# A gated feed-forward layer: four units instead of eight on the leading quarter, and the same four on the second

## The chip, the cores and the metric

The kernel runs on one core of a Trainium2 chip. The metric is the device time of one execution in microseconds (us). Before the change the median of three runs is 299.8 us (299.75 to 299.83).

The engines that matter are TensorE (PE in the profile; PEld are its weight loads), VectorE (DVE), ScalarE (ACT), GpSimd (POOL) and SyncE (SP). SP, ACT and POOL also issue DMAs; each has a queue of its own.

## The reference

`x` is 1024 tokens by 1024, `w_gate` and `w_up` are 1024 by 3584, `w_down` is 3584 by 1024, all in bf16:

```python
def _gelu(x):
    return jax.nn.gelu(x, approximate=True)

def reference(x, w_gate, w_up, w_down):
    return (_gelu(x @ w_gate) * (x @ w_up)) @ w_down
```

## The kernel before, in words

**The work.** The 3584 hidden columns are 28 units of 128. For a unit and a range of tokens, TensorE adds up eight steps over the inner dimension (k 0 to 7), once with gate weights (G) and once with up weights (U). Such a pair is a *part* (list `parts`, line 136). When its G and U are complete, ACT puts the GELU of G into one of four buffers `tb` (line 443), and VectorE multiplies it by U from PSUM into `hT` (line 483). When all units are done, the second product runs 17 jobs over the 28 units (line 421), and ACT and VectorE copy the result out.

**The opening.** The first product needs x with the inner dimension on the partitions, so x is transposed on the chip. Three ways are used:
- Tokens 0 to 255 (`XA`) come as two loads `xa`, one on SP's and one on ACT's queue (line 293). TensorE transposes k 0 to 4 through the identity (`turn_xa`, line 345), ACT copies these from PSUM into `xT` in the four pieces of `XA_PS` (line 436), and VectorE transposes k 5 to 7 in 16 instructions of 32 partitions by 192 (line 459).
- Tokens 256 to 383 (`XB1`), 384 to 511 (`XB2`) and 512 to 1023 (`XC2`) are loaded in runs of 512 bytes into `xs` (line 284), each in four DMAs of 32 partitions, two on SP (side 0) and two on ACT (side 1). VectorE transposes them, one k at a time (line 474).

Units 0 to 7 open together on tokens 0 to 255: eight parts of 256 tokens, one PSUM bank each, walked k by k, so that every k needs one gate and one up piece of 128 rows by 1024 columns (`load_w0`, line 288, 16 DMAs of 256 KB in runs of 2 KB, all on SP). Then the same eight units run on tokens 256 to 511: units 0 to 3 walk k together, its first four k in two strips of 128 tokens, then units 4 to 7 go one after the other. After that come units 0 to 7 on tokens 512 to 1023, and units 8 to 27 on both halves of 512 tokens, one part after the other, each with two PSUM banks.

**Weights after the opening.** They come in groups of four units (`groups`, line 109), 1 MB of gate on SP and 1 MB of up on POOL (`load_w`, line 275), in runs of 1 KB. There are three places for a group: `lo` and `hi`, the two halves of the wide buffer `big` that holds units 0 to 7 at first, and `small`. The first group waits in `gate_w` (line 304) until the last 512 tokens of x have landed, a later one until the units whose place it takes are done. `w_down` is loaded in seven pieces of 1 MB between them (`issue_wd`).

**What sets the order.** Everything is written out by hand: `steps` (line 157) is TensorE's order of multiplications, `dve_order` (line 187) is VectorE's, where `E` is the multiplication of a part and A, B, C and D are the transposes of XB1, XB2, XC2 and the whole of 256 to 511 for one k. ACT's and SP's programs are their loops. An engine works through its list in order, so that a wait in it holds what stands behind. On SP these are `xa`, the 16 first weight pieces, a wait for the up piece of k 5, its six x loads, then the groups. ACT issues `xa`, makes its copies, waits for the same up piece and issues its six x loads; its GELUs stand behind that. `HOLD` (line 132) adds one wait of TensorE for the gate piece of k 7.

Of the kernel before, what the change touches and what calls it, by code (L numbers as in the profile page):

```python
# [5 lines left out]
P = 128  # L6
BF16 = mybir.dt.bfloat16
FP32 = mybir.dt.float32
ACTF = mybir.ActivationFunctionType
# [75 lines left out]
def bass_standalone__geglu_ffn__sampling_kernel(  # L85
# [23 lines left out]
    groups = [(8, 4, "s"), (12, 4, "lo"), (16, 4, "hi"), (20, 4, "s"), (24, 4, "lo")]  # L109
    assert groups[-1][0] + groups[-1][1] == FM  # L110
    NG = len(groups)
    war = [None, 3, 7, 11, 15]
    slot_of = {m: ("lo" if m < GSZ else "hi", m % GSZ, None) for m in range(NBIG)}
# [17 lines left out]
    XA_PS = [(3, 0, 1, 0, 1), (7, 0, 1, 1, 2), (4, 1, 3, 0, 2), (5, 3, 5, 0, 2)]  # L131
    HOLD = ((6, "U", 5), ("wg", 7))
    XA_DVE = (5, 8)
# [3 lines left out]
    for t0, t1 in (XA, XB):  # L137
        for m in range(NBIG):
            parts.append((m, t0, t1, (m, 0, 256), (m, 256, 512)))
    NSHORT = len(parts)  # L140
    rest = [(m, 1) for m in range(NBIG)] + [(m, h) for m in range(NBIG, FM) for h in range(NH)]
    for n, (m, h) in enumerate(rest):
        b = 2 * (n % 4)
        parts.append((m, h * 512, h * 512 + 512, (b, 0, 512), (b + 1, 0, 512)))
# [29 lines left out]
    for key, ps_ in (("G", (0, 1, 2, 6, 3, 7, 4)), ("U", (0, 1, 2, 3)), ("G", (5,)), ("U", (7, 6, 4, 5))):  # L174
        steps += [(p, key, 0, None) for p in ps_]
    together(range(0, 8), 1, 6)
    for half in (range(0, 4), range(4, 8)):
        together(half, 6, 7)
        one_by_one(half, 7)
    together(range(8, 12), 0, 4, XB1)  # L180
    together(range(8, 12), 0, 4, XB2)
    together(range(8, 12), 4, 6)
    one_by_one(range(8, 12), 6)
    one_by_one(range(12, NPART), 0)
# [3 lines left out]
    mix = ("E0 E1 E2 A0 E3 A1 A2 A3 B0 B1 B2 B3 E4 D4 D5 E5 D6 D7 E6 E7 "  # L188
           "C0 E8 C1 E9 C2 E10 E11 C3 C4 E12 C5 E13 C6 C7 E14 E15")
# [5 lines left out]
    dve_order += [("E", p) for p in range(NSHORT, NPART)]  # L195
# [26 lines left out]
    Q_W0 = {(w, k): _Clock(f"{w}0k{k}", 16) for k in range(DK) for w in ("wg", "wu")}  # L222
# [10 lines left out]
    with ExitStack() as es:  # L233
# [54 lines left out]
        def load_w0(ew, eng, w, k):  # L288
            ctx.set((w + "0", k), ew.do(lambda: eng.dma_start(  # L289
                big[w][:, k, :], w_r[w][:, k, 0:NBIG * P]), clock=Q_W0[(w, k)]))  # L290

        def early_loads(ew, eng, side):
            ctx.set(("xa", side), ew.do(lambda: eng.dma_start(  # L293
                xa[:, side, :], xa_r[:, side, :]), clock=Q_XA[side]))
            yield
            if side == 0:
                for k in range(DK):
                    for w in ("wg", "wu"):
                        load_w0(ew, eng, w, k)
            ew.wait(Q_W0[("wu", 5)], ctx.get(("wu0", 5)))  # L300
            for q in XPIECES:
                load_x(ew, eng, q, side)

        def gate_w(ew, j):
            if war[j] is None:
                for s in range(2):
                    ew.wait(Q_X[(XC2, s)], ctx.get(("x", XC2, s)))
                return -1
            ew.wait(C_PE, ctx.get(("U", last_part[war[j]])))
            return war[j]  # L310

        def prog_pool(eng):
            pool = _Eng(ctx, eng, C_POOL)
            v = pool.do(lambda: eng.iota(diff[:, :], pattern=[[1, P]], base=0, channel_multiplier=-1))
            pool.wait(C_POOL, v)
            ctx.set("ident", pool.do(lambda: eng.tensor_scalar(
                ident[:, :], diff[:, :], 0.0, None, ALU.is_equal)))
            wd_mine = [k for k in range(len(wd_groups)) if k % 2 == 1]
            for j in range(NG):
                known_chunk = gate_w(pool, j)  # L320
                load_w(pool, eng, "wu", j)
                issue_wd(pool, eng, wd_mine, known_chunk, Q_WD_POOL)
            issue_wd(pool, eng, wd_mine, FM, Q_WD_POOL, force=True)
            ctx.set("wd_pool_total", Q_WD_POOL.n)

        def prog_sp(eng):
            sp = _Eng(ctx, eng, None)
            for _ in early_loads(sp, eng, 0):
                pass
            wd_mine = [k for k in range(len(wd_groups)) if k % 2 == 0]  # L330
            for j in range(NG):
# [26 lines left out]
        def part_step(pe, eng, opened, i, key, dk, tok):  # L358
# [6 lines left out]
            if j is None:  # L365
                pe.wait(Q_W0[(w, dk)], ctx.get((w + "0", dk)))
# [12 lines left out]
            if (i, key, dk) == HOLD[0]:  # L379
                pe.wait(Q_W0[HOLD[1]], ctx.get((HOLD[1][0] + "0", HOLD[1][1])))  # L380
# [48 lines left out]
        def prog_act(eng):  # L429
            act = _Eng(ctx, eng, C_ACT)  # L430
            act.do(lambda: eng.activation(warm[:, 0:1], const0, ACTF.Gelu_apprx_tanh))
            for _ in early_loads(act, eng, 1):
                for j, (bank, k0, k1, b0, b1) in enumerate(XA_PS):
                    act.wait(C_PE, ctx.get(("XP", j)))
                    nt = P * (b1 - b0)
                    ctx.set(("XA", j), act.do(lambda: eng.activation(  # L436
                        xT[:, k0:k1, P * b0:P * b1],
                        ps[:, bank, 0:nt * (k1 - k0)].rearrange("p (k t) -> p k t", t=nt), ACTF.Copy)))
            for i, (m, t0, t1, (gb, g0, g1), us) in enumerate(parts):
                act.wait(C_PE, ctx.get(("U" if us[0] == gb else "G", i)))  # L440
# [100 lines left out]
```

## Time and profile before

| what | us or share |
|---|---|
| median of three runs | 299.8 |
| the profiled execution | 299.5 |
| its span in the profile | 298.2 |
| TensorE busy | 295.0 (99%) |
| VectorE busy | 64.2 (22%) |
| ACT busy | 42.3 (14%) |
| first multiplication with weights starts | 4.85 |
| units 0 to 7 are through tokens 0 to 255 | 19.37 |
| units 0 to 7 are through tokens 256 to 511 | 33.42 |
| second product starts | 199.18 |

Times inside the profile count from the start of its span. Matmuls overlap their neighbours, so the distance between two starts, and not the length of one, is what a matmul costs. A line of the timeline gives start, length, engine, line of the kernel, operation, tiles and how many instructions were merged; in brackets stands the idle time before it and what ended it. In the rows by stage, the busy time of PE, PEld, DVE, ACT and POOL is followed by the clock, the mean share of the 16 DMA engines and GB/s. A DMA's landing is counted from its issue.

### The profile page before, as it was taken

What the parts mean: (1) busy time and instruction counts of PE and PEld (TensorE: products, weight loads), DVE (VectorE), ACT (ScalarE), POOL (GpSimd) and SP (SyncE); (2) the same over time, 40 slices, a digit from 0 to 9 for tenths busy, and PEclk for the clock granted to TensorE, in tenths of its full rate; (3) what the DMA queues carried; (4) which work ended last, traced back from release to release, by engine and by line L of the source; (5) the groups of instructions that cost most, each with busy time, mean ns of one, the idle gap of its engine ahead of it and who ended that gap; (6) DMA issues with size and microseconds to landing.
All of it is one profiled execution on the core that took longest, in us unless ns stands there. A gap on an engine that the chain in (4) does not pass through costs nothing.

```text
span 298.2 us, 3516 instructions
## 1 busy us (share of the span) xinstructions
PE 295.0 (99%) x1552; PEld 148.9 (50%) x1552; DVE 64.2 (22%) x108; ACT 42.3 (14%) x79; POOL 7.8 (3%) x14
## 2 busy tenths in 40 slices
PE   8999999999999999999999999999999999999997
PEld 5889644444444444444444444444444444444446
DVE  4669721111122111122111122110000000000000
ACT  4032211121111121111121111110000000000000
POOL 1001001020000002001000000000000000000000
DMA  7988004856009301943104000000000100010001
GB/s 256 393 198 266 19 2 138 284 191 235 0 0 297 127 0 29 370 166 99 44 0 141 0 2 0 0 0 20 18 18 20 35 18 18 20 35 18 18 20 35
DMA packets 17806, 26.43 MB, mean 89 GB/s; under 512 B 1024, under 2 KB 11392, under 8 KB 17792
## 3 DMA queue, kind: packets, MB, share of 16 engines
q1 hardware_dynamic: 13840, 16.78, 17.0%
q0 software_dynamic: 2176, 8.39, 8.0%
q10 hardware_dynamic: 1776, 1.05, 1.3%
q8 instruction: 12, 0.20, 0.3%
q14 instruction: 2, 0.02, 0.0%
HBM read 24.12 MB, written 2.10 MB: 88 GB/s over the span
## 4 chain that ended last, share of the span: by engine, by line
PE 94%; DMA 3%; SPq 2%; issue 0%; ACT 0%
PE ps L384 61%; PE ps L421 32%; DMA wubig<-in_w_up_dram 3%; SPq L289 2%; SPq L293 0%; ACT xT L449 0%
## 5 line engine op out<-in xcount | busy, mean ns | idle before, releaser
L421 PE MATMUL ps<-wd,hT 128*128 128x512 bf16 (+1 forms) x476 | 96.9, 367 | 0.0
L384 PE MATMUL ps<-xT,wgbig 128*128 128x512 bf16 (+2 forms) x400 | 79.8, 337 | 0.2 <-DMA wgbig<-in_w_gate_dram 0.2
L384 PE MATMUL ps<-xT,wubig 128*128 128x512 bf16 (+2 forms) x400 | 79.8, 337 | 0.2
L421 PEld LDWEIGHTS ps<-wd,hT 128*128 128x128 bf16 x476 | 46.5, 98 | 50.5
L483 DVE TENSOR_TENSOR hT<-tb,ps 128x512 bf16<-128x512 f32 (+1 forms) x64 | 38.9, 613 | 136.6 <-PE ps L384 136.6
L443 ACT ACTIVATE tb<-ps 128x512 f32<-128x512 f32 (+1 forms) x64 | 34.1, 544 | 158.5 <-PE ps L384 157.0
L384 PEld LDWEIGHTS ps<-xT,wubig 128*128 128x128 bf16 x400 | 38.0, 98 | 32.2 <-DMA wubig<-in_w_up_dram 0.7
L384 PEld LDWEIGHTS ps<-xT,wgbig 128*128 128x128 bf16 x400 | 38.0, 98 | 31.6 <-DMA wgbig<-in_w_gate_dram 0.3
L384 PE MATMUL ps<-xT,wusmall 128*128 128x512 bf16 x128 | 30.2, 379 | 0.0
L384 PE MATMUL ps<-xT,wgsmall 128*128 128x512 bf16 x128 | 30.2, 379 | 0.0
L489 DVE CAST xT<-ps 128x512 bf16<-128x512 f32 (+1 forms) x8 | 5.3, 658 | 88.1 <-PE ps L421 88.1
L384 PEld LDWEIGHTS ps<-xT,wusmall 128*128 128x128 bf16 x128 | 12.5, 98 | 15.1
L384 PEld LDWEIGHTS ps<-xT,wgsmall 128*128 128x128 bf16 x128 | 12.5, 98 | 15.1
L449 ACT ACTIVATE xT<-ps 128x512 bf16<-128x512 f32 (+1 forms) x9 | 5.2, 573 | 93.1 <-PE ps L421 93.1
L474 DVE STREAM_TRANSPOSE xT<-hT 128x128 bf16<-128x128 bf16 (+2 forms) x20 | 13.3, 706 | 0.0
L459 DVE STREAM_TRANSPOSE xT<-hT 32x192 bf16<-32x192 bf16 x16 | 8.2, 514 | 4.6 <-DMA hT<-in_x_dram 4.1
L278 POOL DMA_DIRECT2D wubig<-in_w_up_dram x3 | 2.7, 884 | 63.4 <-PE ps L384 63.4
L398 PE MATMUL ps<-const-bfloat16-1.0 128*128 128x512 bf16 (+1 forms) x10 | 3.1, 502 | 0.8 <-PEq L526 0.8
L278 POOL DMA_DIRECT2D wusmall<-in_w_up_dram x2 | 2.0, 990 | 47.2 <-PE ps L384 26.0
L272 POOL DMA_DIRECT2D wd<-in_w_down_dram x3 | 2.3, 762 | 19.1 <-PE ps L384 19.1
L398 PEld LDWEIGHTS ps<-const-bfloat16-1.0 128*128 128x128 bf16 x10 | 1.3, 142 | 2.4 <-issue 2.4
L436 ACT ACTIVATE xT<-ps 128x128 bf16<-128x128 f32 (+1 forms) x4 | 1.5, 438 | 1.9 <-PE ps L351 1.8
(10 smaller groups left out, 4.4 us busy)
## 6 DMA issues: line engine op xcount, KB each, us to landing
wd<-in_w_down_dram SPq DMA_DIRECT2D x4, 1024.0 KB, 11.3
wgbig<-in_w_gate_dram SPq DMA_DIRECT2D x3, 1024.0 KB, 5.7
wubig<-in_w_up_dram POOLq DMA_DIRECT2D x3, 1024.0 KB, 9.8
wd<-in_w_down_dram POOLq DMA_DIRECT2D x3, 1024.0 KB, 11.5
wgbig<-in_w_gate_dram SPq DMA_DIRECT2D x8, 256.0 KB, 5.5
wubig<-in_w_up_dram SPq DMA_DIRECT2D x8, 256.0 KB, 5.7
wgsmall<-in_w_gate_dram SPq DMA_DIRECT2D x2, 1024.0 KB, 6.1
wusmall<-in_w_up_dram POOLq DMA_DIRECT2D x2, 1024.0 KB, 9.7
```

What stands on the lines that cost most here:

```text
L272: ew.do(lambda: eng.dma_start(wd[:, a:b, :], wd_r[:, a:b, :]), clock=clock)
L278: ctx.set((w, j), ew.do(lambda: eng.dma_start(wbuf(w, buf)[:, :, 0:gsz * P], w_r[w][:, :, c0 * P:(c0 + gsz) * P]), clock=q))
L289: ctx.set((w + "0", k), ew.do(lambda: eng.dma_start(big[w][:, k, :], w_r[w][:, k, 0:NBIG * P]), clock=Q_W0[(w, k)]))
L384: v = pe.do(lambda: eng.matmul(ps[:, bank, f0:f1], wbuf(w, buf)[:, dk, slot * P:(slot + 1) * P], xT[:, dk, t0:t1], start=first, stop=last ...
L398: pe.do(lambda: eng.matmul(ps[:, 0, 0:n], ones_w, ones_x[:, 0:n], start=True, stop=True), mark=False)
L421: v = pe.do(lambda: eng.matmul(ps[:, b, 0:ncols], hT[:, m, tc * P:(tc + 1) * P], wd[:, m, col0:col0 + ncols], start=(m == 0), stop=(m == F ...
L443: ctx.set(("A", i), act.do(lambda: eng.activation(t_bufs[i % NTB][:, 0:t1 - t0], ps[:, gb, g0:g1], ACTF.Gelu_apprx_tanh)))
L449: ctx.set(("E", ji), act.do(lambda: eng.activation(osb[:, tc, col0:col0 + ncols], ps[:, b, 0:ncols], ACTF.Copy)))
L459: v = dve.do(lambda: eng.transpose(xT[32 * a:32 * (a + 1), XA_DVE[0]:XA_DVE[1], XA[0]:XA[1]].rearrange("p k (b t) -> p k b t", t=P)[:, :, ...
L474: v = dve.do(lambda: eng.transpose(xT[:, dk, q[0]:q[1]].rearrange("p (c i) -> p c i", i=32), src))
L483: ctx.set(("D", i), dve.do(lambda: eng.tensor_tensor(hT[:, m, t0:t1], t_bufs[i % NTB][:, 0:t1 - t0], ps[:, ub, u0:u1], ALU.mult)))
L489: ctx.set(("E", ji), dve.do(lambda: eng.tensor_copy(osb[:, tc, col0:col0 + ncols], ps[:, b, 0:ncols])))
```

## The change

Four units open instead of eight. Units 0 to 3 run on tokens 0 to 255 in PSUM banks 0 to 3, then on tokens 256 to 511 in banks 4 to 7; of these only k 0 is in two strips of 128 tokens. Units 4 to 7 have no short parts any more: they run on tokens 0 to 511 whole, one part after the other. Then the order goes on as before.

The first weights are 512 columns wide, for four units, in runs of 1 KB, and come in five pieces of gate and of up each: k 0, k 1, k 2-3, k 4-5 and k 6-7. Units 4 to 7 become a group of their own (index 0, place `hi`), with gate and up both on SP, right behind SP's pieces of XB1 and XB2 and ahead of its pieces of XC2. SP has no wait in this stretch any more. ACT waits for the gate piece of k 4-5, issues its pieces of XB1 and XB2, and issues those of XC2 after its first four GELUs. TensorE transposes k 0 to 6 of the first tokens (14 instead of 10 transposes, with a fifth piece in bank 6 for ACT to copy), and VectorE only k 7. `HOLD` is gone, and `dve_order` is written anew. POOL begins with group 1.

```diff
-    groups = [(8, 4, "s"), (12, 4, "lo"), (16, 4, "hi"), (20, 4, "s"), (24, 4, "lo")]
+    groups = [(4, 4, "hi"), (8, 4, "s"), (12, 4, "lo"), (16, 4, "hi"), (20, 4, "s"), (24, 4, "lo")]
-    war = [None, 3, 7, 11, 15]
+    war = [None, None, 3, 7, 11, 15]
...
-    XA_PS = [(3, 0, 1, 0, 1), (7, 0, 1, 1, 2), (4, 1, 3, 0, 2), (5, 3, 5, 0, 2)]
-    HOLD = ((6, "U", 5), ("wg", 7))
-    XA_DVE = (5, 8)
+    XA_PS = [(3, 0, 1, 0, 1), (7, 0, 1, 1, 2), (4, 1, 3, 0, 2), (5, 3, 5, 0, 2), (6, 5, 7, 0, 2)]
+    XA_DVE = (7, 8)
+    W0 = [(0, 1), (1, 2), (2, 4), (4, 6), (6, 8)]
...
-    for t0, t1 in (XA, XB):
-        for m in range(NBIG):
-            parts.append((m, t0, t1, (m, 0, 256), (m, 256, 512)))
+    for t0, t1, b0 in (XA + (0,), XB + (GSZ,)):
+        for m in range(GSZ):
+            parts.append((m, t0, t1, (b0 + m, 0, 256), (b0 + m, 256, 512)))
...
-    rest = [(m, 1) for m in range(NBIG)] + [(m, h) for m in range(NBIG, FM) for h in range(NH)]
+    rest = [(m, 0, 512) for m in range(GSZ, NBIG)] + [(m, 512, 1024) for m in range(NBIG)]
+    rest += [(m, h * 512, h * 512 + 512) for m in range(NBIG, FM) for h in range(NH)]
...
-    for key, ps_ in (("G", (0, 1, 2, 6, 3, 7, 4)), ("U", (0, 1, 2, 3)), ("G", (5,)), ("U", (7, 6, 4, 5))):
-        steps += [(p, key, 0, None) for p in ps_]
-    together(range(0, 8), 1, 6)
-    for half in (range(0, 4), range(4, 8)):
-        together(half, 6, 7)
-        one_by_one(half, 7)
-    together(range(8, 12), 0, 4, XB1)
-    together(range(8, 12), 0, 4, XB2)
-    together(range(8, 12), 4, 6)
-    one_by_one(range(8, 12), 6)
-    one_by_one(range(12, NPART), 0)
+    for k0, k1 in W0:
+        for key in ("G", "U"):
+            for dk in range(k0, k1):
+                steps += [(p, key, dk, None) for p in range(GSZ)]
+    together(range(GSZ, NSHORT), 0, 1, XB1)
+    together(range(GSZ, NSHORT), 0, 1, XB2)
+    together(range(GSZ, NSHORT), 1, DK)
+    one_by_one(range(NSHORT, NPART), 0)
...
-    mix = ("E0 E1 E2 A0 E3 A1 A2 A3 B0 B1 B2 B3 E4 D4 D5 E5 D6 D7 E6 E7 "
-           "C0 E8 C1 E9 C2 E10 E11 C3 C4 E12 C5 E13 C6 C7 E14 E15")
+    mix = ("A0 B0 D1 D2 E0 D3 E1 D4 E2 D5 E3 D6 D7 E4 E5 E6 E7 "
+           "C0 C1 E8 C2 C3 E9 C4 C5 C6 E10 C7 E11")
...
+        def load_w0(ew, eng, w, i):
+            k0, k1 = W0[i]
+            ctx.set((w + "0", i), ew.do(lambda: eng.dma_start(
+                wbuf(w, "lo")[:, k0:k1, :], w_r[w][:, k0:k1, 0:GSZ * P]), clock=Q_W0[(w, i)]))
...
-            for _ in early_loads(sp, eng, 0):
-                pass
+            load_xa(sp, eng, 0)
+            for i in range(len(W0)):
+                for w in ("wg", "wu"):
+                    load_w0(sp, eng, w, i)
+            load_x(sp, eng, XB1, 0)
+            load_x(sp, eng, XB2, 0)
+            load_w(sp, eng, "wg", 0)
+            load_w(sp, eng, "wu", 0)
+            load_x(sp, eng, XC2, 0)
             wd_mine = [k for k in range(len(wd_groups)) if k % 2 == 0]
-            for j in range(NG):
+            for j in range(1, NG):
...
+            act.wait(Q_W0[("wg", 3)], ctx.get(("wg0", 3)))
+            load_x(act, eng, XB1, 1)
+            load_x(act, eng, XB2, 1)
             for i, (m, t0, t1, (gb, g0, g1), us) in enumerate(parts):
+                if i == GSZ:
+                    load_x(act, eng, XC2, 1)
                 act.wait(C_PE, ctx.get(("U" if us[0] == gb else "G", i)))
```

## The prediction

> **What bounds the kernel now.** I read the shares of the engines and the chain that ended last first, then the timeline of TensorE at the start, then the waits up to 60 us, then the DMA issues with their landings and the rate of each kind of transfer.
>
> From the page, shares and chain:
>
> ```profile
> PE 295.0 (99%) x1552; PEld 148.9 (50%) x1552; DVE 64.2 (22%) x108; ACT 42.3 (14%) x79; POOL 7.8 (3%) x14
> ...
> PE 94%; DMA 3%; SPq 2%; issue 0%; ACT 0%
> ```
>
> TensorE is the chain from 16.85 us to the end. So only idle time of TensorE counts, and it lies in the first 17 us. The timeline of TensorE (start, length, count, idle before):
>
> ```profile
> 3.77 0.94 PE L351 MATMUL ps<-ident,hT 128*128 128x128 bf16 x10
> 4.85 0.94 PE L384 MATMUL ps<-xT,wgbig 128*128 128x256 bf16 x7 [0.15 <-DMA wgbig<-in_w_gate_dram]
> 5.87 0.61 PE L384 MATMUL ps<-xT,wubig 128*128 128x256 bf16 x4
> 8.62 1.04 PE L384 MATMUL ps<-xT,wgbig 128*128 128x256 bf16 x8
> 9.49 1.04 PE L384 MATMUL ps<-xT,wubig 128*128 128x256 bf16 x8
> 16.85 0.28 PE L384 MATMUL ps<-xT,wubig 128*128 128x256 bf16 x1
> 19.37 0.39 PE L384 MATMUL ps<-xT,wgbig 128*128 128x128 bf16 x4
> 19.59 0.39 PE L384 MATMUL ps<-xT,wubig 128*128 128x128 bf16 x4
> 33.42 1.89 PE L384 MATMUL ps<-xT,wgbig 128*128 128x512 bf16 x8
> 35.15 1.89 PE L384 MATMUL ps<-xT,wubig 128*128 128x512 bf16 x8
> ```
>
> Starts, not lengths, give the pace: 0.87/8 = 0.109 us for 256 columns, 0.22/4 = 0.056 for 128, 1.73/8 = 0.216 for 512. At 33.42 units 0 to 7 are done on tokens 0 to 511. From 4.85, 128 multiplications of 256 columns would take 13.96 us, but the second quarter begins at 19.37: 14.52. So 0.56 us is lost to two waits for up weights (before 5.87 and 16.85). The wait list shows them on the weight loads (us, times, longest):
>
> ```profile
> PEld ps L384 <- DMA wubig<-in_w_up_dram: 0.7, 2, 0.4
> PEld ps L384 <- DMA wgbig<-in_w_gate_dram: 0.3, 1, 0.3
> ```
>
> Rates by stage (PE, PEld, DVE, ACT, POOL busy, clock, DMA share, GB/s). First weights in 2 KB runs, then a group in 1 KB runs beside another queue, then x in 512 B runs:
>
> ```profile
> 8.00:11.00 3.00, 3.00 (x30) 2.70 (x28) 2.84 (x6) 0.00 (x0) 0.00 (x0) 1.00 1.05 405
> 25.00:29.00 4.00, 4.00 (x39) 3.58 (x38) 3.98 (x7) 1.92 (x5) 0.00 (x0) 1.00 1.08 373
> 18.00:21.00 3.00, 3.00 (x45) 2.85 (x43) 3.00 (x12) 1.59 (x6) 0.00 (x0) 1.00 1.14 270
> ```
>
> Per full share that is 385, 345 and 237 GB/s. Four x issues (timeline), and the landing of the second ACT piece:
>
> ```profile
> 13.20 0.45 ACTq L284 DMA_DIRECT2D hT<-in_x_dram  x1
> 14.59 1.53 SPq L284 DMA_DIRECT2D hT<-in_x_dram  x1
> 16.16 0.58 ACTq L284 DMA_DIRECT2D hT<-in_x_dram  x1
> 16.16 0.54 SPq L284 DMA_DIRECT2D hT<-in_x_dram  x1
> ```
>
> ```profile
> hT<-in_x_dram ACTq DMA_DIRECT2D x1, 64.0 KB, 4.4
> ```
>
> **The change, part by part.** Equal work is compared at before's 33.42.
>
> 1. *Shapes.* Four units on tokens 0-255: 64 x 0.109 = 6.98 us. Four on 256-511: 16 x 0.056 + 56 x 0.109 = 7.00. Units 4-7 whole: 64 x 0.216 = 13.80. Sum 27.78; from a start at 4.85 that ends at 32.63, 0.79 ahead of 33.42. Of this 0.56 is the two waits gone and 0.23 is fewer narrow multiplications. From there to the end the order and widths are the old ones.
>
> 2. *Start.* Four more transposes of x on TensorE: (0.94-0.23)/9 = 0.08 each, 0.32 us. Ten ended their starts at 4.47, so fourteen free TensorE at about 4.87, against 4.85. Cost 0, because TensorE waited for weights there (0.29 idle on the weight load); uncovered it would be 0.32. The fifth copy on ACT (0.6 us) ends near 6.2 and is needed only at k 5, near 9.2. VectorE gets 32x64 instead of 32x192 transposes. At the 0.38 of the 128x128 row, which is twice as long per partition, 16 x 0.41 from 4.1 end at 10.7, and k 7 is needed near 11. Cost 0.
>
> 3. *First weights.* The need per microsecond is unchanged (half the weights, half the work), but 1 KB runs go at 345 instead of 385. I shift old landings of equal cumulative bytes by that 10% on the weights' part. Up to 768 KB (old first gate piece, 1.17+3.6 = 4.8): the first up piece near 4.85, needed 5.29. Gate k 2-3 at 1280 KB: old 2.10+4.5 = 6.6, now 6.8, needed 6.6: 0.2 late. Gate k 4-5 at 1792 KB: old 3.05+5.0 = 8.05, now 8.4, needed 8.54 with that delay. The last up piece: 8.4 + 3 x 0.76 = 10.7, needed 11.15. Cost 0.2; bounds 0 (2 KB pace) and 0.6 (a repeat of what is lost now). After it everything would be on time. First quarter ends near 12.03.
>
> 4. *x for tokens 256-511.* SP issues its pieces right behind the weights, near 6, without its old wait of 3.8 us; ACT waits for gate k 4-5 (8.4) and then issues four at 0.45 us: 8.4, 8.85, 9.3, 9.75. Behind that wait on ACT stand only GELUs not due before 11.6. Old landings were 3.3, 4.4, 3.2 and 4.1 us after issue, with an instruction fetch on one DMA engine at 14.8 (queue 8: 12 packets, 0.3% of 16 engines' 298 us, so 1.2 us each). Without it the last pieces take about 2.9 to 3.2: first half landed near 11.9, second 12.65. Bytes agree: 0.52 MB at 237-255 after 10.7 is 12.7-12.9. VectorE transposes the first strip in 0.4: 12.3, against 12.03, 0.3 late. The second strip ends at 13.1, against 12.3+0.45: 0.35 late. Afterwards VectorE needs 0.54+0.29 per k against TensorE's 0.87: it keeps up. Cost 0.6; bounds 0 (the x data interleaves and lands in 2.6) and 2.0 (landings of 4.4).
>
> 5. *Units 4-7.* Their weights leave POOL's and the 2 KB loads and go on SP in two 1 MB pieces right behind x; SP's half of the last 512 tokens is queued behind them, ACT's after four GELUs near 13. Up weights land: 12.7 + 2.1 MB/345 (6.1) + ACT's 0.52 MB of x (2.1) = 20.9, or 22.1 on the engine that fetches instructions. Needed: 4.85+13.98+0.8+1.73 = 21.4. Cost 0.1; bounds 0 and 0.7. The last x lands near 22.5 as now (SP's next group went out at 22.29), needed from 32; the next groups on SP and POOL wait for it as before and are used near 60: 0.
>
> Sum: -0.79 + 0.2 + 0.6 + 0.1 = +0.1. Two of my choices (4, 5) are on the late side and share their delay, so I take -0.1. The profiled execution was 299.5 (span 298.2 and 1.3 around it), the median of the runs 299.8; the change goes from the median: 299.7.
>
> [...]
>
> **The rivals.**
>
> *B, everything is on time.* The x pieces and weights arrive before they are needed, because 768 KB of weights are still open when ACT issues x, and before it was 1 MB. Only the shapes and the old waits count: 299.8 - 0.79 = 299.0. For it: every lateness above is under 0.4 us. Against: 1 KB and 512 B rates. [...]
>
> *C, ACT's x issues are held behind SP's large issues* (slower). At 14.59 SP's and ACT's issues of 256 KB took 1.53 and 1.49 us and ended together; the next pair took 0.54 and 0.58. Issues can thus be held on both queues at once when much is queued. Now SP issues two 1 MB pieces near 8 to 9, exactly when ACT must issue x. One hold of 0.95 us makes x 0.95 later: 299.7 + 0.95 = 300.7. If a piece of x has to wait till a whole 1 MB piece has drained (1.05 MB/345 = 3.0 us): 302.7. Taken at 301.2. It decides once ACT's four issues take over 3 us instead of 1.8. Against: sixteen weight pieces were issued without a hold. [...] No row before shows one issuer alone holding the other.
>
> *D, the up weights of units 4-7 are late* through the x of ACT and the instruction fetch: 22.1 or later against 21.4, another 0.6 over the forecast: 300.3. For it: margins under 1 us. Against: a later second quarter moves the need too.
>
> **How the numbers follow.** Forecast A (299.7, alone 299.1 to 300.3): 0.45, of which 0.07 is under 299.2, 0.35 within 0.6 us and 0.03 over 300.4. B 0.14, all faster. C 0.26, all slower. D 0.15: 0.04 within and 0.11 slower. Bound: 0.2% is 0.6 us, about what a measurement of this kernel can tell from no change. Faster 0.07+0.14 = 0.21; within 0.35+0.04 = 0.39; slower 0.03+0.26+0.11 = 0.40. The range 299.0 to 301.8 leaves out some of B (0.06) and the upper half of C (0.13).
>
> **What would show it.** Part 1: 64, then 16 narrow and 56, then 64 wide multiplications, the wide ones beginning 0 to 0.8 us ahead of 33.42 less 13.80, that is 18.8 to 19.6. Part 2: first weights' multiplication at 4.8 to 4.9. Part 3: idle of TensorE for weights before 12 us of about 0.2. Part 4: idle for VectorE's transposes of about 0.6 between 12 and 13.5; over 1.5 with ACT issues above 1 us is C; none is B. Part 5: idle for the up weights near 21 of at most 0.2. The prediction is wrong if the second quarter begins later than 13, or if anything after 34 us changes its length (165.9 us of the first product's 512-wide work and 96.8 of the second).

## The result, and the profile after

The changed kernel takes 308.64 us (median of five runs, 307.45 to 310.25) against 299.83 for the kernel before (five runs, 299.75 to 300.47) on the same chip: a ratio of 1.0295, 95% interval 1.0271 to 1.0318. It is slower by 8.8 us, where 299.7 was forecast. The profiled execution took 310.25, with a span of 308.9. All of this execution's difference lies in the first 44 us:

| what, in us from the start of the span | before | after |
|---|---|---|
| first multiplication with weights | 4.85 | 5.44 |
| tokens 256 to 511 begin | 19.37 | 17.90 |
| first 512-wide multiplication (units 4 to 7 begin) | | 30.35 |
| units 0 to 7 through tokens 0 to 511 | 33.42 | 44.16 |
| second product starts | 199.18 | 209.92 |

From the fourth row to the fifth both kernels need 165.76 us. The loss is 44.16 - 33.42 = 10.74 us in this execution. (The record of the first 512-wide multiplication is missing from the trace; 30.35 is the start of the second, 30.56, less one pace of 0.216.)

From the page: shares, the granted clock in 40 slices of 7.7 us, and the chain that ended last.

```profile
PE 298.1 (96%) x1442; PEld 145.0 (47%) x1468; DVE 60.6 (20%) x101; ACT 42.3 (14%) x76; POOL 7.9 (3%) x14
...
PEclk9957999999999999999999999999999999999999
...
PE 92%; DMA 5%; SPq 1%; issue 1%; ACTq 0%; DVE 0%; ACT 0%; DVEq 0%
```

TensorE's busy time rose by 3 us although the change takes narrow multiplications away, its share fell from 99% to 96%, and the clock dips in the third and fourth slice. So there are two kinds of loss: waits, and multiplications that run slower. The timeline shows where (start, length, engine, line, operation, tiles, count, and in brackets the idle time before and what ended it):

```profile
5.44 0.96 PE L383 MATMUL ps<-xT,wgbig 128*128 128x256 bf16 x4
6.24 0.60 PE L383 MATMUL ps<-xT,wubig 128*128 128x256 bf16 x4
...
8.41 0.62 SPq L277 DMA_DIRECT2D wgbig<-in_w_gate_dram  x1
...
9.07 1.05 SPq L277 DMA_DIRECT2D wubig<-in_w_up_dram  x1
9.15 2.74 ACTq L283 DMA_DIRECT2D hT<-in_x_dram  x4
...
17.44 0.40 DVE L478 STREAM_TRANSPOSE xT<-hT 128x128 bf16<-128x128 bf16 x1 [8.11 <-DMA hT<-in_x_dram]
17.90 0.61 PE L383 MATMUL ps<-xT,wgbig 128*128 128x128 bf16 x4 [3.97 <-DVE xT L478]
...
21.09 0.61 PE L383 MATMUL ps<-xT,wgbig 128*128 128x128 bf16 x4 [2.16 <-DVE xT L478]
...
21.92 1.06 PE L383 MATMUL ps<-xT,wgbig 128*128 128x256 bf16 x4
22.77 1.06 PE L383 MATMUL ps<-xT,wubig 128*128 128x256 bf16 x4
```

The four x issues of ACT go out from 9.15, right behind SP's two issues of 1 MB (8.41 and 9.07). VectorE then waits 8.11 us for that x, TensorE 3.97 for VectorE, and 2.16 more for the second strip. Behind the wait four multiplications of 256 columns take 0.85 (22.77 - 21.92) instead of the 0.44 of before. The list of waits up to 60 us (us, times, longest) names x and hardly the weights:

```profile
DVE xT L478 <- DMA hT<-in_x_dram: 10.9, 2, 8.1
PEld ps L383 <- DVE xT L478: 6.7, 2, 4.3
...
PEld ps L383 <- DMA wgbig<-in_w_gate_dram: 1.1, 2, 0.7
...
PEld ps L383 <- DMA wubig<-in_w_up_dram: 0.2, 1, 0.2
```

The rows by stage (busy time of PE, PEld, DVE, ACT and POOL, clock, DMA share, GB/s) show 309 GB/s instead of 405 from 8 to 11 us, where the last first weights and SP's first x move, and the clock at half:

```profile
8.00:11.00 3.00, 3.00 (x30) 2.70 (x28) 1.20 (x5) 0.00 (x0) 0.00 (x0) 1.00 1.08 309
16.50:17.00 0.50, 0.00 (x0) 0.00 (x0) 0.00 (x0) 0.00 (x0) 0.00 (x0) 0.50 1.10 263
24.00:26.00 2.00, 2.00 (x12) 1.39 (x10) 1.94 (x5) 0.00 (x0) 0.00 (x0) 0.50 0.25 55
```

Added up against the 32.63 at which the forecast's shapes would end without any wait (4.85 + 27.78):

| loss of the profiled execution | us | from |
|---|---|---|
| later start | 0.6 | 5.44 - 4.85 |
| first four multiplications at half pace | 0.4 | 6.24 - 5.44 = 0.80 against 0.44 |
| waits for first weights | 1.0 | the first quarter's last multiplication starts at 13.65 and ends its 0.11 at 13.76: 8.32 after 5.44, less 6.98 and the row above |
| x for the first strip | 4.1 | 17.90 - 13.76 |
| x for the second strip | 2.4 | gap of 2.47 between starts, less the pace |
| half clock | 3.1 | 30.35 - 17.90 - 2.36 = 10.09, against 7.00 |
| units 4 to 7 | 0.0 | 44.16 - 30.35 = 13.81, against 13.80 |

Unrounded that is 11.5, and 32.63 + 11.5 = 44.1. Some 9.6 of it hangs on x: 6.5 of waits, and 3.1 of a clock that fell to 0.50 at 16.41, within TensorE's 3.97 us of idle time, and came back at 26.65; it stayed at 1.00 there in the run below in which the idle time is filled. These losses add up to more than the 8.8 of the medians, since the profiled execution is the slowest of the five: the other four have a mean clock of 0.989 instead of 0.983, which over 307 us is an estimated 6.8 us at half clock against 10.24 here.

Where was x? Packets by DMA queue from 11 to 13 us (q1 is SP's, q10 ACT's; packets, MB, share of 16 engines):

```profile
q1 hardware_dynamic: 430, 0.34, 103.9%
q10 hardware_dynamic: 9, 0.00, 1.3%
...
hT<-in_x_dram ACTq DMA_DIRECT2D x1, 64.0 KB, 10.0
```

ACT had issued 256 KB of x, 512 packets of 512 B, by 11.9; nine packets moved by 13, the first of them 3.2 us after ACT's first issue. The pieces landed at 16.0, 17.4, 17.9 and 20.5, that is 6.8 to 10.0 us after their issue, where the kernel before had 3.2 to 4.4. SP's own four pieces, which stand ahead of the group on SP's queue, were late too: they landed 4.6 to 6.7 us after their issue, at 11.2 to 14.2.

### The profile page after: what moved, and what is told of

The parts are those of the page before. It is cut to its first block, busy times and chain, and to the rows that moved or that the text cites. A ratio compares the mean times of both kernels' runs of the same rounds, so it can differ in the third digit from the quotient of the medians.

```text
span 308.9 us, 3299 instructions
## 1 busy us (share of the span) xinstructions
PE 298.1 (96%) x1442; PEld 145.0 (47%) x1468; DVE 60.6 (20%) x101; ACT 42.3 (14%) x76; POOL 7.9 (3%) x14
## 3 DMA queue, kind: packets, MB, share of 16 engines
q1 hardware_dynamic: 15824, 16.78, 17.9%
## 4 chain that ended last, share of the span: by engine, by line
PE 92%; DMA 5%; SPq 1%; issue 1%; ACTq 0%; DVE 0%; ACT 0%; DVEq 0%
PE ps L383 61%; PE ps L420 31%; DMA hT<-in_x_dram 3%; DMA wgbig<-in_w_gate_dram 2%; SPq L289 1%; ACTq L283 0%; DVE xT L478 0%; SPq L293 0%; ACT xT L453 0%; DVEq L41 0%
## 5 line engine op out<-in xcount | busy, mean ns | idle before, releaser
L383 PE MATMUL ps<-xT,wgbig 128*128 128x512 bf16 (+2 forms) x347 | 78.6, 365 | 7.1 <-DVE xT L478 6.1
L383 PE MATMUL ps<-xT,wubig 128*128 128x512 bf16 (+2 forms) x354 | 78.9, 364 | 0.1
L383 PEld LDWEIGHTS ps<-xT,wgbig 128*128 128x128 bf16 x356 | 35.3, 101 | 42.7 <-DVE xT L478 6.7
L383 PEld LDWEIGHTS ps<-xT,wubig 128*128 128x128 bf16 x356 | 35.6, 101 | 35.5 <-DMA wubig<-in_w_up_dram 0.2
L453 ACT ACTIVATE xT<-ps 128x512 bf16<-128x512 f32 (+1 forms) x9 | 5.2, 574 | 93.1 <-PE ps L420 93.1
L478 DVE STREAM_TRANSPOSE xT<-hT 128x512 bf16<-128x512 bf16 (+2 forms) x17 | 13.1, 802 | 10.9 <-DMA hT<-in_x_dram 10.9
L463 DVE STREAM_TRANSPOSE xT<-hT 32x64 bf16<-32x64 bf16 x16 | 4.6, 284 | 4.8 <-DMA hT<-in_x_dram 4.3
L435 ACT ACTIVATE xT<-ps 128x512 bf16<-128x512 f32 (+1 forms) x5 | 2.2, 468 | 2.2 <-PE ps L352 2.0
```

What stands on the lines that cost most here:

```text
L383: v = pe.do(lambda: eng.matmul(ps[:, bank, f0:f1], wbuf(w, buf)[:, dk, slot * P:(slot + 1) * P], xT[:, dk, t0:t1], start=first, stop=last ...
L453: ctx.set(("E", ji), act.do(lambda: eng.activation(osb[:, tc, col0:col0 + ncols], ps[:, b, 0:ncols], ACTF.Copy)))
L463: v = dve.do(lambda: eng.transpose(xT[32 * a:32 * (a + 1), XA_DVE[0]:XA_DVE[1], XA[0]:XA[1]].rearrange("p k (b t) -> p k b t", t=P)[:, :, ...
L478: v = dve.do(lambda: eng.transpose(xT[:, dk, q[0]:q[1]].rearrange("p (c i) -> p c i", i=32), src))
```

## The experiments

Unless said otherwise an edit is to the changed kernel. Every ratio is to the kernel before, with a 95% interval.

**The group of units 4 to 7 behind x.** SP issues the two 1 MB pieces only when all of x for tokens 256 to 511 has landed.

```diff
             load_x(sp, eng, XB2, 0)
+            for q in (XB1, XB2):
+                for s in range(2):
+                    sp.wait(Q_X[(q, s)], ctx.get(("x", q, s)))
             load_w(sp, eng, "wg", 0)
```

> Change: SP waits until all pieces of x for tokens 256 to 511 have landed before it issues the two 1 MB pieces of units 4 to 7. Theory 1 (ACT's x pieces stood behind SP's two large pieces: issued from 9.15 us, landed at 16.0 to 20.5): x then lands about 4 us after ACT's issues, the last near 13 to 14.5, TensorE waits 0.3 to 1.5 us for it instead of 4.0 and 2.2, the clock stays at 1.00, and the time is 299 to 301.5. Rival 2 (the pieces in 512-byte runs are slow by themselves in this stage, or ACT's wait is what makes them late): they land after 16 again, the clock drops again, and the time stays over 306.

304.80 us, ratio 1.0169 (1.0153 to 1.0186). ACT's x, issued at 9.29 to 10.62, landed at 12.2 to 13.8, that is 2.6 to 3.8 us after issue. The same window from 11 to 13 us now reads:

```profile
q10 hardware_dynamic: 487, 0.22, 50.1%
q1 hardware_dynamic: 129, 0.06, 15.9%
```

The wait of 3.97 us became 0.69, and the clock stayed at 1.00. So the group ahead is what made ACT's x this late: undoing that one order shows it. (SP's last x, which stands behind the group on SP's queue, moves back with it.) The total was missed by over 3 us, because the group, now issued at 13.8 and 14.5, was late in its turn:

```profile
13.99 0.40 PE L386 MATMUL ps<-xT,wgbig 128*128 128x128 bf16 x4 [0.69 <-DVE xT L481]
...
22.95 1.90 PE L386 MATMUL ps<-xT,wgbig 128*128 128x512 bf16 x8 [1.79 <-DMA wgbig<-in_w_gate_dram]
...
26.75 1.90 PE L386 MATMUL ps<-xT,wubig 128*128 128x512 bf16 x8 [1.90 <-DMA wubig<-in_w_up_dram]
```

**The idle time filled.** Multiplications of zeros by ones, which add nothing to the result, keep TensorE busy in both gaps, 18 of 512 columns in the first and 42 of 128 in the second. The tile of zeros and the lines that multiply it are left out here.

```diff
...
+    steps += [("F", True)] * 18
     together(range(GSZ, NSHORT), 0, 1, XB1)
+    steps += [("F", False)] * 42
     together(range(GSZ, NSHORT), 0, 1, XB2)
...
```

> Change: the two waits of TensorE for x (4.0 and 2.2 us) are filled with multiplications by a zero weight tile, 18 of 512 columns ahead of the first strip and 42 of 128 columns ahead of the second; nothing else. Theory 2 (the waits cost twice: TensorE idles, and then works at half the clock from 16.5 to 26.7 us because it idled): x lands as late as before, but the granted clock stays 1.00 through 14 to 28 us, so the second quarter's 7.0 us of work take 7 instead of about 10.5, and the time falls by 3 to 4 us to 304.5 to 306. If the half clock has another cause, it comes anyway and the time stays within 0.7 of 308.6.

307.56 us, ratio 1.0240 (1.0212 to 1.0268). x was as late as before (landed 15.8 to 19.5), but the clock stayed at 1.00 in the stretch where it had been 0.50, and the pace agrees:

```profile
24.00:26.00 2.00, 2.00 (x21) 1.78 (x20) 0.97 (x2) 0.00 (x0) 0.00 (x0) 1.00 0.12 28
```

From the second strip to the first 512-wide multiplication it needed 28.06 - 21.50 = 6.56 us instead of 30.35 - 21.09 = 9.26: the half clock cost 2.7 us there. From profile to profile 2.2 of these 2.7 reached the total (310.25 to 308.06); the second filling ran about 1.4 us past the point at which x was ready. From median to median it is 1.1, so that the 3 to 4 us that I had expected were missed; they had been worked out from the 10.24 us of half clock in the one profile.

**All of x on SP, ahead of the group.** ACT issues none of tokens 256 to 511.

```diff
-            load_x(sp, eng, XB1, 0)
-            load_x(sp, eng, XB2, 0)
+            for q in (XB1, XB2):
+                for s in range(2):
+                    load_x(sp, eng, q, s)
...
-            act.wait(Q_W0[("wg", 3)], ctx.get(("wg0", 3)))
-            load_x(act, eng, XB1, 1)
-            load_x(act, eng, XB2, 1)
```

> Change: SP issues all eight pieces of x for tokens 256 to 511 itself, right behind the first weights and ahead of the two 1 MB pieces; ACT issues none of them and does not wait. Theory 1: order on the queue is what counts, so x lands near 12.5 to 14.5 although the 1 MB pieces follow at once; time 299 to 301.5. Rival 2 (slow in this stage anyway): landing after 16, time over 306. A third one, that much in one queue slows every transfer (the rate fell to 161 to 222 GB/s between 10 and 13 us): landing 14.5 to 16 and 302 to 305.

302.25 us, ratio 1.0082 (1.0059 to 1.0105). On one queue x came ahead of the group issued behind it, though its pieces did not land in the order of their issue (the second at 13.2, the third at 12.0): x landed at 11.3 to 15.0, the group, issued at 10.4 and 11.1, at 19.4 and 24.9. The clock stayed at 1.00. TensorE's waits are many and short: six of 0.3 to 0.9 us (between starts) from 6 to 15 us, for first weights and x, and 0.84 for the up weights of units 4 to 7 at 24.9. The third of the expected ranges, 302 to 305 with a landing of 14.5 to 16, is the one that came, though its reason was not tested: with x out from behind the group some 2.4 us are still missing.

**The same hold in the kernel before.** There SP issues x and then both 1 MB pieces of its first group ahead of its last x; ACT's issues are untouched, and SP's wait for the up piece of k 5 is gone.

```diff
+            if side == 0:
+                load_x(ew, eng, XB1, 0)
+                load_x(ew, eng, XB2, 0)
+                load_w(ew, eng, "wg", 0)
+                load_w(ew, eng, "wu", 0)
+                load_x(ew, eng, XC2, 0)
...
```

> The kernel before with one thing of the change: SP issues its x pieces for tokens 256 to 511 right behind the first weights and then both 1 MB pieces of its first group, before its last x pieces; ACT issues x where it did. Still eight units, 2 KB runs. Theory 1: ACT's x pieces (issued near 12.8) stand behind the two large ones and land 6 us or more after their issue, near 19 to 22 instead of 16.1 to 18.3; TensorE, which needs the first of them at 19.4, waits 1 to 3 us, so 300.5 to 303. Rival 2: x lands as before within 1 us and the time stays within 0.6 of 299.8.

304.72 us, ratio 1.0174 (1.0139 to 1.0210). ACT's x landed 6.5 to 7.6 us after issue instead of 3.2 to 4.4, and TensorE waited 1.97 us for the transposes at 21.19. The first fence is this kernel from 15 to 17 us, in which ACT's queue moved nothing, the second the kernel before:

```profile
q1 hardware_dynamic: 653, 0.48, 114.9%
```

```profile
q1 hardware_dynamic: 442, 0.20, 42.0%
q10 hardware_dynamic: 455, 0.21, 41.8%
```

So the hold needs neither four units nor first weights in runs of 1 KB. The loss was larger than expected because the last 512 tokens of x were late as well (landed at 29.7; three more waits between 36 and 40 us).

**One 1 MB piece ahead.** Gate ahead of ACT's x, up behind the landing of x (the three waiting lines of the first experiment, moved between the two loads).

> The changed kernel with only the gate piece (1 MB) of units 4 to 7 ahead of ACT's x; SP waits for all x of tokens 256 to 511 before it issues the up piece. Theory 1 in its plain form (ACT's x stands behind what SP has issued before it): half the bytes ahead, half the delay. With both pieces ahead the last x landed at 20.5, with none at 13.8; so here near 16 to 18, and TensorE waits about 2 to 3 us for it. If one piece of 1 MB fits without holding ACT, x lands by 14.5, and the loss moves to the up weights alone.

307.27 us (one run). ACT's x landed at 16.1 to 19.3, nearly as late as with two pieces ahead (16.0 to 20.5). Half the bytes took away little of the lateness, as far as one run can say.

**Narrow runs alone, in the kernel before.** The wide buffer is laid out in two halves, so that the 16 first pieces move in runs of 1 KB instead of 2 KB; order and everything else stay.

```diff
-        big = {w: sb(w + "big", [P, DK, NBIG * P], BF16) for w in ("wg", "wu")}
+        big = {w: sb(w + "big", [P, 2, DK, GSZ * P], BF16) for w in ("wg", "wu")}
...
```

> The kernel before with the two halves of its wide weight buffer apart, so that the same 16 first pieces of 256 KB go in runs of 1 KB instead of 2 KB; nothing else. Theory 3 (runs of 1 KB cost about 0.80 us per 256 KB where 2 KB cost 0.66): the last up piece lands at 18.0 to 19 instead of 16.8, the second quarter begins 0.5 to 1.2 us after 19.4, time 300.3 to 301. [...]

300.16 us (ten runs), ratio 1.0028 (1.0015 to 1.0041). From 7 to 15 us a piece of 256 KB lands every 0.75 us instead of 0.68. The row that was 405 GB/s:

```profile
8.00:11.00 3.00, 3.00 (x30) 2.67 (x29) 2.81 (x7) 0.00 (x0) 0.00 (x0) 1.00 1.09 355
```

The direction was right and the size somewhat smaller than expected. Runs of 1 KB cost 0.6 us (by the medians) to 0.8 (by the ratio) with 4 MB in them; the change has 2 MB.

**The last x later.** To the kernel with the group behind x: ACT issues its pieces of tokens 512 to 1023 after eight GELUs instead of four, so that they do not move beside the group.

```diff
-                if i == GSZ:
+                if i == NSHORT:
                     load_x(act, eng, XC2, 1)
```

> The kernel of the run in which SP waits for x, with one thing more: ACT issues its pieces of the last 512 tokens after eight GELUs (near 20 us) instead of four (13.4). Theory 4 (the new waits for the weights of units 4 to 7, 2.06 and 2.27 us, come from these 512 KB running beside them): gate lands near 19.5 to 20.5 and up near 22 to 23 instead of 22.9 and 26.7, the two waits shrink to under 1 us together, time 300.5 to 301.5. If they come from the late issue at 13.8 alone, the waits stay over 3 us together and the time over 303.5.

302.78 us, ratio 1.0110 (1.0088 to 1.0133). The two waits for the group, 2.06 and 2.27 us between starts, shrank to about 0 and 0.3, as that theory said. 2.0 of the 3.9 us came through, so that the time lies between the two expected ranges; a new wait of 1.43 for the transposes of the last x at 37.7 and longer waits for the last first weights (0.85) and for x (1.41) took the rest. Up to x this kernel is the one with the group behind x, and yet ACT's x landed at 13.2 to 15.3, 3.4 to 5.1 us after issue instead of 2.6 to 3.8: two traces of the same opening differ by 0.8 to 1.4 us. Nothing of the group was issued before 15.35, and still the engines moved little from 11 to 13 us, with all 16 busy:

```profile
11.00:13.00 2.00, 1.59 (x13) 0.94 (x11) 0.00 (x0) 0.00 (x0) 0.00 (x0) 1.00 1.15 158
```

The kernel with 1 KB runs alone has 348 GB/s in this window. What makes the transfers slow there, with the last first weights in 1 KB runs and x in 512 B runs mixed, was not tested.

**x earlier.** To that kernel: ACT issues x one weight piece earlier (it waits for the gate piece of k 2-3 instead of k 4-5).

> The same with ACT waiting for the gate piece of k 2 and 3 (landed 7.7) instead of k 4 and 5 (9.3), so that x is issued 1.5 us earlier. If x is what holds the second quarter there, it lands near 12.5, the wait of 0.96 us for it goes, the group is issued 1.3 us earlier and its waits go: 299.6 to 300.5. If x only takes bandwidth from the last first weights, these land later by what x gains and the time stays within 0.4 of the run beside it.

302.51 us, ratio 1.0094 (1.0073 to 1.0115). x, issued at 7.1 to 8.5, landed at 11.8 to 13.2, and the wait for it fell to 0.91, but only 0.3 us reached the total. The expected 299.6 to 300.5 was missed. The time is the one of the other theory, but not its reason: the last first weights landed at 11.4, earlier than the 13.2 of the kernel beside it.

**The group on POOL.** The two 1 MB pieces go out on POOL (at 7.35 and 8.44, 1.1 and 0.6 us earlier than on SP), to see whether x is still late when SP's queue does not carry them.

```diff
         def prog_pool(eng):
...
+            pool.wait(Q_W0[("wg", 2)], ctx.get(("wg0", 2)))
+            load_w(pool, eng, "wg", 0)
+            load_w(pool, eng, "wu", 0)
...
-            load_w(sp, eng, "wg", 0)
-            load_w(sp, eng, "wu", 0)
+            sp.wait(Q_WG[0], ctx.get(("wg", 0)))
             load_x(sp, eng, XC2, 0)
```

> Edit to the changed kernel: the two 1 MB pieces of units 4 to 7 are issued by POOL instead of SP, at the same time (once the gate piece of k 2-3 has landed, near 8 us); SP issues its last x pieces once the 1 MB of gate has landed. ACT's x issues are as in the changed kernel. Theory 5 (SP's and ACT's queues share one path on which SP's 1 MB pieces stand ahead of ACT's x; POOL's queue does not use it): ACT's pieces land 3 to 5 us after their issue (12.5 to 14.5 us), the second quarter begins with a wait of at most 1.2 us, the clock stays full, and the time is 300 to 303.5, what is left being the rate of narrow runs and the group's own landing. Rival (any 2 MB ahead in the DMA engines hold x, whoever issued them): ACT's pieces land 6 to 10 us after issue (16 us and later), TensorE waits about 4 us near 14, and the time is 306 to 310.

311.39 us, ratio 1.0391 (1.0374 to 1.0409), the slowest of all. ACT's four issues took 1.79 us together, without any hold, and yet their x landed at 17.2 to 22.5, 8 to 12 us after issue. TensorE stood still for 8.3 us from 13.7 on. So x was late with the group off SP's queue too, and theory 5 fell. The packets tell more. From 15 to 17 us (q0 is POOL's), in the second fence the changed kernel from 19 to 21, and in the third the changed kernel from 13 to 16:

```profile
q0 software_dynamic: 153, 0.61, 91.2%
q10 hardware_dynamic: 152, 0.07, 14.4%
```

```profile
q1 hardware_dynamic: 421, 0.33, 67.5%
q10 hardware_dynamic: 422, 0.21, 50.3%
```

```profile
q1 hardware_dynamic: 759, 0.76, 91.3%
q10 hardware_dynamic: 285, 0.13, 18.4%
```

In the first two windows both queues moved nearly the same number of packets (153 and 152, 421 and 422), though these carried different amounts: 0.61 MB in 153 packets is 4.0 KB each, against 0.5 KB of x. The kernel before in its window above has 442 against 455, and there both carry x. Beside POOL's group x then got a tenth of the bytes in that window (0.07 of 0.68 MB). Other windows show no equal counts: in the third SP's queue moved 2.7 times as many packets as ACT's (759 and 285), though all of ACT's x for tokens 256 to 511 had been issued, with the group on POOL the counts from 18 to 20 us are 30 (POOL) and 616 (ACT), and in the changed kernel from 11 to 13 us they were 430 (SP) and 9 (ACT). How a DMA engine chooses between the queues is not shown.

**POOL, with x earlier.** To the kernel with x earlier: the group on POOL as above, and the last x of SP and ACT issued when the gate weights of units 4 to 7 have landed.

> The same with three more edits: ACT issues its pieces of tokens 256 to 511 one weight piece earlier, and SP and ACT both issue their last x pieces as soon as the gate piece of units 4 to 7 has landed. Theory 5: x for the second quarter lands by 13.5, the group by 17 and 21, the last x by 26, no wait over 0.6 us, and the time is 299.0 to 301. Rival: as the one before, 304 to 308, since x issued at 7 us also stands partly behind the group.

307.25 us, ratio 1.0236 (1.0193 to 1.0279). POOL's issues were at 7.47 and 8.56, ACT's four at 7.19, 7.56, 8.17 and 8.65. They landed 5.1, 7.1, 8.7 and 10.0 us later, against 4.7, 5.1, 4.6 and 4.8 without POOL's: the first, issued ahead of POOL's, hardly lost, and each one lost more than the one before it. This agrees with the runs above: in them too x landed late when the group had been issued before it, behind 2 MB on SP's queue 6.5 to 10.0 us after issue, with 2 MB on POOL's 8.1 to 12.0.

**Half a megabyte ahead.** To the kernel with the group behind x: only k 0 to 3 of the gate weights (512 KB) go ahead of x.

```diff
             load_x(sp, eng, XB2, 0)
+            load_w(sp, eng, "wg", 0, 0, 4)
...
-            load_w(sp, eng, "wg", 0)
+            load_w(sp, eng, "wg", 0, 4, DK)
```

> Edit to the kernel of the experiment with the group behind x: only the first half of units 4 to 7's gate weights (k 0 to 3, 512 KB in one issue) goes out on SP ahead of ACT's x; the other half and the up weights still wait until x has landed. Theory 6 (the DMA engines take what was issued earlier first, whichever queue issued it, at about 345 GB/s, so that 1 MB ahead costs 3.0 us and 512 KB 1.5): ACT's x pieces land 1.3 to 2.2 us later than with the group behind (12.3, 13.5, 12.7, 13.8 there), that is 4.0 to 5.8 us after their issue; the wait of the second quarter grows from 0.7 to 2.0 to 2.9, the waits for the group shrink, and the time is 302.5 to 304.5. Rival (one large issue ahead holds x, whatever its size): x lands 6.5 us or more after its issue, as behind 1 MB, and TensorE waits about 4 us; 305 to 308.

306.71 us, ratio 1.0239 (1.0208 to 1.0271). x landed 5.8, 7.4, 5.7 and 7.1 us after issue, and TensorE stood still for 3.6 us before the second quarter. Against the first trace with nothing of the group ahead that is 2.8 to 3.9 later, against the second (the kernel with the last x later) 2.0 to 2.6. Strict order at 345 GB/s made 1.5, with 1.3 to 2.2 as its range, and "any large issue" made 6.5 or more after issue for every piece, which two of the four pieces do not reach. So the rival fell by its landings, though its 305 to 308 came; the time of strict order, 302.5 to 304.5, was missed, and the landings, one trace each, do not decide on it. The landings of ACT's x for tokens 256 to 511, for the runs in which all of it was issued behind the group or without it:

| issued ahead of or beside ACT's x | lands after issue, us |
|---|---|
| nothing of the group, ACT's wait as in the change (two kernels) | 2.6 to 3.8, and 3.4 to 5.1 |
| nothing of the group, x one weight piece earlier (two kernels) | 4.4 to 5.3 |
| 512 KB on SP | 5.7 to 7.4 |
| 1 MB on SP | 6.6 to 8.5 |
| 2 MB on SP (the change, with the gaps filled, and in the kernel before) | 6.5 to 10.0 |
| 2 MB on POOL, 4 KB packets, all of it ahead | 8.1 to 12.0 |

The steps between 0.5, 1 and 2 MB are small against the step from nothing to 0.5 MB; no run shows why. In the 512 KB run ACT's own last x, issued at 14.6, also moved beside the two pieces that landed last. Why ACT's first packet moves only 3.2 us after its issue in the change, 3.5 behind 512 KB and 5.4 beside POOL, against 1.0 and 1.2 in the two kernels of the first row, stays open.

**The last x when the gate weights land.** To the kernel with x earlier and the last x later: ACT's last pieces wait for the gate weights of units 4 to 7 instead of for the eighth GELU.

> Edit to the kernel with x earlier and the last x later: ACT issues its last x pieces as soon as the gate weights of units 4 to 7 have landed (near 19.1) instead of after its eighth GELU (20.65). If the 1.14 us that TensorE waited at 36 for the last transposes came from that lateness, it goes, while the wait for the up weights near 22 grows from 0.45 to at most 1.0: 301.0 to 302.0, still slower than before. If the transposes themselves are what is late (8 of 1.05 us and 4 multiplications between 27.2 and 36.9), at most 0.5 of it goes: 302.0 to 302.5.

301.84 us, ratio 1.0087 (1.0062 to 1.0113): the lowest median of all forms of the changed kernel (with all x on SP, 302.25, it overlaps), and still slower than before. The time lies in the first expected range, but the wait for the last transposes went only from 1.14 to 0.88 between starts, as the second one had it; so lateness of the last x explains little of that wait. The clock did not fall after the start, and the remaining waits are these:

```profile
5.38 0.60 PE L386 MATMUL ps<-xT,wgbig 128*128 128x256 bf16 x4
...
7.64 1.05 PE L386 MATMUL ps<-xT,wgbig 128*128 128x256 bf16 x8 [0.35 <-DMA wgbig<-in_w_gate_dram]
...
13.78 0.40 PE L386 MATMUL ps<-xT,wgbig 128*128 128x128 bf16 x4 [0.72 <-DVE xT L482]
...
20.80 1.89 PE L386 MATMUL ps<-xT,wgbig 128*128 128x512 bf16 x8
22.94 1.90 PE L386 MATMUL ps<-xT,wubig 128*128 128x512 bf16 x8 [0.25 <-DMA wubig<-in_w_up_dram]
...
37.21 0.39 PE L386 MATMUL ps<-xT,wgbig 128*128 128x512 bf16 x1 [0.50 <-DVE xT L482]
```

By distances between starts, less the pace: start 0.53 later than 4.85, first weights 0.51, x 0.89, up weights 0.41, last x 0.66. That is 3.00 against the 0.79 that the shapes gain, or +2.2; its span is 300.5 against 298.2. Much of the 0.53 goes with a clock that came up late in this execution (last section): its transposes stand 0.107 apart up to 5.3 us, where 0.062 is the full pace.

## Why the prediction was wrong

**Step 1, shapes: right.** The last form above needs 20.80 - 13.78 = 7.02 us for the second quarter (7.00 forecast); the changed kernel needs 13.81 for units 4 to 7 (13.80 forecast). The 0.79 is there.

**Step 2, start: right where the clock is up, 0.6 otherwise.** Forecast 0, measured 0.6 in the profiled execution, and 0.4 more for four multiplications at half pace. All fourteen traces begin at half pace (0.43 us for 512 columns up to 3.3 us, 0.216 later), and the pace doubles between 3.4 and 6.5 us (last section); in this one it does so at 6.17. In the four traces of the changed kernel's forms with the full pace by 4.5 us the first multiplication starts at 4.85 to 5.20, mean 5.01; in the three of the kernel before and its forms, all with the full pace by then, at 4.85 to 5.09, mean 5.01. In the other seven, where the clock came later, the mean is 5.38. So no cost of the four transposes shows; the forecast had no term for the clock at the start. Whether the change makes a late clock more frequent is not shown.

**Step 3, first weights: mis-sized.** Forecast 0.2, with 0.6 as the upper bound, measured 1.0, and 0.5 in the best form. Runs of 1 KB are about as slow as I took them (0.75 us a piece against 0.76). What I left out is that SP's x, issued right behind without the old wait of 3.8 us, moves beside the last weights in runs of 512 B: the rate was 309 GB/s against 355 in the kernel with 1 KB runs alone, and the last up piece landed at 12.8, not 10.7.

**Step 4, x for tokens 256 to 511: this is where it failed.** Forecast 0.6, bounds 0 and 2.0; measured 6.5. I took the landing of an x piece from the kernel before, 2.9 to 3.2 us after issue, and counted only the bytes of x after the last weights. The 2 MB that SP issues just ahead of ACT's x stood in step 5, as something that comes after x. With it ahead the landings were 6.8 to 10.0; with it out of the way 2.6 to 3.8 in one trace, near the forecast, and 3.4 to 5.1 in another, and the wait for x fell from 6.5 to 0.9 and 1.3 us less the pace.

**Step 4 had the rate of x wrong as well.** It took 237 to 255 GB/s, from a stage in which x moves alone. Behind the first weights, with no group ahead, the rate from 11 to 13 us was 158 in the kernel with the last x later, at a DMA share of 1.15, that is 137 per full share. In line with this, SP's second piece of the first strip landed at 12.7 and 13.8 in the two kernels with the group behind x, where 11.9 was forecast. The cause of this rate stays open.

**Step 4 had no term for the clock.** Behind the long wait for x (3.97 us) the work ran slower, at a clock of 0.50: 2.7 us by the filled gaps, 3.1 by the sum. No bound of mine held it.

**Step 5, units 4 to 7: right by luck.** In the changed kernel they cost nothing, because everything else was later still. The up weights landed at 24.8, not 20.9, with ACT's last x, issued at 13.97 and 14.32, on its way beside them. When x was mended they cost 3.9 us (2.06 + 2.27 less the pace of two starts), or 0.4 when the last x was moved away. Step 5's 0 for the last x was also wrong: 0.7 to 1.2 in the last three mended kernels, less the pace.

**Rival C had the place and the kind, not the price.** It was given 0.26 and 300.7 to 302.7, by "a whole 1 MB piece has drained", 3.0 us. Its sign was wrong too: it was to decide once ACT's four issues take over 3 us. They took 2.74 with a loss of 6.5, and 1.79 with POOL, where the loss was largest. The time was lost between issue and landing (6.8 to 10.0 and 8.1 to 12.0 us), not in the issue. Rivals B and D did not come about in the changed kernel.

**What was to make the prediction wrong** was a second quarter that begins later than 13 (it began at 17.90) or another length after 34 us (165.76 in both). The first came, the second did not. The range of 299.0 to 301.8 held x late by at most 2 us; the best mended form, 301.84, lies just outside it.

## What to carry to other kernels

Issue a small urgent load before the bulk, and let the bulk wait for its landing, as the best form here does (301.84 us): with 2 MB on another queue, POOL's, x landed 8.1 to 12.0 us after issue, and 0.5 MB ahead already made it land 2 to 4 us later. Price a landing with everything that has been issued by then on any queue, not with the landing of the same piece in a quieter stage. In these traces the five idle times of TensorE of 3.4 us or more were each followed by a half clock of 3.41 or 10.24 us, and those of up to 2.0 at full clock by none, so a bound on a long wait has to include that.

## What the hardware showed that was not expected

**The half clock came in pieces of one length, on a grid.** A trace keeps the times at which the granted clock changed. In the changed kernel it was 0.50 from 16.41 to 26.65, 10.24 us; with the group on POOL from 16.39 to 26.63, again 10.24. It lasted 3.41 us from 18.07 with 512 KB ahead, from 18.44 with 1 MB ahead, and from 20.14 with POOL and x earlier. In each trace the distances between changes are whole multiples of 3.41: from the first change, at 6.17 in the changed kernel and 4.42 to 6.49 in the others, to the drop they are 10.24 or 13.65. Counted off from the first change in windows of 3.41 us, each of the five traces has its drop at the end of a window, and the idle time inside that window was 2.5 to 3.4 us; windows with 1.9 us or less of idle time at full clock brought no drop. The clock came back at the end of a window with at most 0.7 us of idle time, and not with 1.3. With POOL and x earlier the drop, at 20.14, came 1.0 us after TensorE had started again (idle from 15.8 to 19.2), again at the end of a window. Nor was a window ahead of a drop always idle from end to end: in the changed kernel TensorE was idle for 2.5 of the 3.41 us up to 16.41. What sets this length is not shown.

**Two queues moved equal numbers of packets in some windows** while they carried packets of different size (421 and 422 with 1 and 0.5 KB mixed, 153 and 152 with 4 and 0.5 KB), but other windows of the same runs have 759 and 285, and 30 and 616.

**The first multiplications at half pace.** In the changed kernel fourteen transposes and four multiplications up to 6.2 us ran at 0.11 and 0.20 us each, half the pace of before, while the rows by stage show a clock of 1.00 there. That 1.00 is not a measurement: the trace's first record of the clock, 1.00, stands at 6.17, just where the pace doubles, and ahead of it there is none. The same holds in all eight traces with such a record at the start (3.51 to 6.49). The other six, the kernel before among them, have no record of the clock at all and show 1.00 throughout; there the pace has to tell. The warm-up multiplications of 512 columns up to 3.3 us are about 0.43 apart in all fourteen traces, the kernel before included, twice the 0.216 of later. So all fourteen executions began at half the later pace, and the time at which it doubled differed from one to the next, from 3.4 to 6.5 us.
